# The last FFN block of an attention, MoE and FFN kernel: squares on VectorE, other places for weight splits, g splits and token rows

## The chip, the cores and the metric

The kernel runs on one core of a Trainium2 chip. The metric is device time in microseconds of one execution; lower is better. Engines are called PE (TensorE), DVE (VectorE), ACT (ScalarE), POOL (GpSimd) and SP (SyncE, which here only issues transfers).

## What is computed

Three stages follow one another: windowed attention with 8 heads over 4 x 576 tokens, a top-2 mixture of 8 experts over the 2304 rows of 512, and an FFN over the same rows:

```python
def _moe2_ref(x, w_in, w_out):       # x: 2304 x 512, w_in: 512 x 2048, w_out: 2048 x 512
    h = x @ w_in
    r = np.maximum(h, 0.0)
    g = r * r
    return (g @ w_out).astype(np.float32)
```

In the mixture, each row goes through two experts `relu(x @ w1[e]) @ w2[e]` and the two results are added with weights; this sum is the x of the FFN.

## The kernel before

A float32 product is made of three passes over two parts of each operand: a high part (a rounded copy) and a low part (operand minus high part). Making these two parts is called a split: ACT writes the high part, DVE or POOL the low part. The FFN's two products use a scheme with seven products of sums and differences in place of eight; P1 to P7 name them.

**FFN's first product** runs over three blocks `s` of 768 rows, and in each over eight pairs `k` of column groups. A pair is seven products (`mul_in`, line 968), each of six matmuls of 384 columns. Their order is P1, P2, P6, P5, P7, then P3 of the pair before (`finish_c`, line 1075), then P4. PE adds P1, P6, P7 and P4 into one PSUM tile `a`; ACT reads it between them (lines 1088, 1094, 1099, and 1107 with its relu), and the next product into `a` waits for the read. `g_sum` (line 989) adds an ACT copy to another PSUM tile on DVE (line 991), takes relu and square, and sends the piece to DRAM (`gmid`). In the last block the relu and square of the sums with `q` 2 and 3 are two ACT instructions (lines 993, 994); all others are one DVE instruction (line 996). There are three PSUM tiles with tag a, two with tag b, one with tag c, handed out in turn.

**Work beside it** is put down by step: `step()` (line 1068) runs after each seventh of a pair and does what `on(slot, ...)` registered. 56 slots make a block, and `end` is the slot after the last block. In the last block this is:

- `w_sums(k, 1)` (line 817), the output weights of pair `k`, in six steps: own copy (ACT, 768 columns), own subtraction (DVE), two additions (DVE), two additions (DVE), rest copy (ACT), rest subtraction (POOL) with the next load of raw weights on SP, which waits for it. Line 1055 places them. They overwrite the input weights of the same pair, already used.
- `g_load`, `g_adds`, `g_split` (lines 1005 to 1030): the first batches of g rows for the second product. A batch is loaded from DRAM, POOL makes four sums, and four parts of a split (ACT, DVE, ACT, DVE) write it into one of three places (`GC`) that held the x operands of the first product. Part 1 also issues the load of the batch three later. Lines 1063 to 1065 place the parts of batches 0 and 1.

**FFN's second product** (`mul_out`, line 1120): 36 batches, each two pairs of seven products of three matmuls with 256 columns; a step follows each product. The output weights of pairs 6 and 7 and further g batches are still being split during its first four batches.

**The last expert** stands ahead of the first block. Its first product (`mm1_a`, eight steps `f`) and second product (`mm2`, row tiles `j` 2 to 4) have the FFN's first rows between them: `ygather` (POOL fetches a row tile's two expert results from DRAM), `combine` (ACT scales one, DVE adds the other), `x2_in` (PE transposes, ACT writes). Dictionaries `C_AT` (by `f`, line 943) and `M_AT` (by step of `mm2`, line 954) place them. `y_out` (line 736) copies an output sum from PSUM; the sums are in tiles of tag b, as are the transposes of `x2_in(..., "b")`.

The order on each engine is that of the program: nothing is reordered, and an instruction that waits holds up all behind it on its engine.

Of the kernel before, what the change touches and what calls it, by code (L numbers as in the profile page):

```python
# [16 lines left out]
AF = mybir.ActivationFunctionType  # L17
OP = mybir.AluOpType
# [30 lines left out]
def attn_moe_ffn(ctx: ExitStack, tc: tile.TileContext, qt, kt, vt, wgn, noise, w1, w2, w_in, w_out,  # L49
                 consts, out):  # L50
    nc = tc.nc
# [10 lines left out]
    slots = dram.tile([NS + 2 * N, 1], I32, name="slots")  # L62
# [8 lines left out]
    def bank(tag):  # L71
        if tag == "b":
            return psum.tile([128, 2, 512], F32, name="psb", tag="b", bufs=2)
        return psum.tile([128, 512], F32, name="ps" + tag, tag=tag, bufs={"a": 3, "c": 1}[tag])
# [408 lines left out]
    def out_a(e, f):  # L483
        relu(PA.pop(f), HA[e][:, f, 0, :], HA[e][:, f, 1, :])
# [21 lines left out]
    for p in range(NT // 2):  # L506
        v = 4 * p + 3
        end = v == last
# [85 lines left out]
    for g in range(4):  # L594
        for d in range(4):
            k, q = 4 * (g % 2), (0, 1, 3, 2)[2 * (g // 2) + d // 2]
            pieces.append((w_in[d * 128:(d + 1) * 128, g * 512:(g + 1) * 512],
                           win32[k:k + 4, :, q, d % 2, :].rearrange("k p n -> p k n"), 4))
    for c in range(16):
        q = slice(0, 4, 3) if c < 8 else slice(1, 3)  # L600
# [50 lines left out]
    def ygather(i):  # L651
        for k in range(2):
            YR[i, k] = rows.tile([128, DM], F32, name="yr", tag="r", bufs=6)
            nc.gpsimd.indirect_dma_start(  # L654
                out=YR[i, k], out_offset=None, in_=yg,
                in_offset=bass.IndirectOffsetOnAxis(ap=pos[:, i, k:k + 1], axis=0))
# [71 lines left out]
    def mm2(e, j, f, py):  # L728
        wc = chunks[8 * e + 4 + f // 2]
        wsl = slice((f % 2) * 512, (f % 2) * 512 + 512)  # L730
        b, m = in_b(e, j)
        h = (HB if b else HA)[e][:, f, :, m * 128:(m + 1) * 128]
        for n, (hq, wp) in enumerate(((0, 0), (0, 1), (1, 0))):
            nc.tensor.matmul(py, h[:, hq], wc[wp][:, wsl], start=(f + n == 0), stop=(f == 7 and n == 2))  # L734
# [22 lines left out]
    def settle(*names):  # L757
        for n in names:
            if n == "wb":
                t = lay("wb")  # L760
                WP[0:2] = [[(0, spot(t, 3584 * m, 7))] for m in range(2)]
            elif n == "xb":
                late["xb"] = lay("xb", F32)
                late["xq"] = late["xb"].rearrange("p (q h c n) -> p q h c n", q=2, h=2, c=2)
            elif n == "wc":
                late["wc"], late["ex"] = lay("wc"), lay("ex")
                at_ = [(late["wc"], m) for m in range(5)] + [(late["ex"], m) for m in range(2)]
                for m, (t, o) in zip((0, 1, 5, 3, 6, 4, 2), at_):
                    XC[m] = t[:, 1536 * o:1536 * (o + 1)].rearrange("p (s c n) -> p s c n", s=2, c=2)
            elif n == "tt":  # L770
                tt, wt = lay("tt", F32), lay("wt", F32)
                tmp.extend([tt[:, 0:HALF], tt[:, HALF:2 * HALF], wt[:, 0:HALF], wt[:, HALF:2 * HALF],
                            late["et"][:, 0:HALF], tt[:, 2 * HALF:3 * HALF]])
            else:
                hb, ha, wa = late["hb"], big["ha"], big["wa"]
                WP[2] = [(0, spot(hb, 0, 7))]
                WP[3] = [(0, spot(big["xa"], 0, 6)), (6, spot(hb, 3584, 1))]
                WP[4] = [(0, spot(ha, 0, 7))]
                WP[5:7] = [[(0, spot(wa, 3584 * m, 7))] for m in range(2)]
                WP[7] = [(0, spot(ha, 3584, 5)), (5, spot(wa, 7168, 2))]  # L780
# [36 lines left out]
    def w_sums(k, out_w, own="dve", rest="pool"):  # L817

        i = 64 + 8 * out_w + k
        st = {}  # L820

        def begin():
            load_to(i + 1)
            r = raws.pop(i).rearrange("p (q n) -> p q n", q=4)
            q = [r[:, n, :] for n in range(4)]
            st["own"], st["add"] = split(WP[k], 0, [r[:, 0:3, :]], own), adds(not out_w, q, q, "dve")
            st["rest"] = split(WP[k], 3, [r], rest)
            do(st["own"][0])

        def end():  # L830
            do(st["rest"][1])
            load_to(i + 3)

        return [begin, lambda: do(st["own"][1]), lambda: do(st["add"][:2]), lambda: do(st["add"][2:]),
                lambda: do(st["rest"][0]), end]
# [104 lines left out]
    settle("xb")  # L940
    for i in range(3):
        ygather(i)
    C_AT = {4: [(combine, 0)], 5: [(x2_in, 0, "b"), (ygather, 3), (combine, 1)],
            6: [(x2_in, 1, "b"), (ygather, 4), (combine, 2)], 7: [(x2_in, 2, "b"), (ygather, 5)]}
    for f in range(8):
        mm1_a(last, f)
        out_a(last, f)
        for g, *a in C_AT.get(f, []):
            g(*a)
        for _ in range(1 + f % 2):  # L950
            if wq:
                wq.pop(0)()
    settle("wc")
    M_AT = {1: [(combine, 3)], 2: [(x_hi, 0)], 3: [(x2_in, 3), (x_lo, 0, "dve")], 4: [(combine, 4)], 5: [(x_hi, 1)],
            6: [(x2_in, 4), (x_lo, 1, "dve")], 8: [(combine, 5)], 10: [(x2_in, 5)], 11: [(x_early, 6)],
            12: [(x_early, 5)], 13: [(x_hi, 5)], 14: [(x_early, 3), (x_lo, 5, "dve")], 15: [(x_hi, 3)],
            16: [(x_lo, 3, "dve"), (x_hi, 6)], 17: [(x_early, 4), (x_lo, 6, "dve")], 19: [(x_hi, 4)],
# [1 line left out]
    for j in range(2, NJ):  # L959
        py = bank("b")[:, 0, :]  # L960
        for f in range(8):
            mm2(last, j, f, py)
            for g, *a in M_AT.get(8 * (j - 2) + f, []):
                g(*a)
# [13 lines left out]
    NSB = N // SB  # L978

    def g_to(s, k, q, t):  # L980
        nc.sync.dma_start(out=gmid[s, k, :, :, q, :].rearrange("u p n -> p u n"),
                          in_=t.rearrange("p (u n) -> p u n", u=3))

    def g_tile():
        ng[0] += 1
        n = (ng[0] - 1) % 4
        return tmp[4 + n // 2] if n % 2 == 0 else rows.tile([128, DM], F32, name="yo", tag="yo", bufs=2)[:, 0:HALF]

    def g_sum(s, k, q, ps, u):
        t = g_tile()  # L990
        nc.vector.tensor_tensor(out=t, in0=ps, in1=u, op=OP.add)  # L991
        if s == NSB - 1 and q:
            nc.scalar.activation(out=t, in_=t, func=AF.Relu)
            nc.scalar.activation(out=t, in_=t, func=AF.Square)
        else:
            nc.vector.scalar_tensor_tensor(out=t, in0=t, scalar=0.0, in1=t, op0=OP.max, op1=OP.mult)
        g_to(s, k, q, t)


# [34 lines left out]
    def on(slot, f, *a):  # L1034
        side.setdefault(slot, []).append((f, a))

    def on_all(slots, steps):
        for m, f in zip(slots, steps):
            on(m, f)
# [3 lines left out]
    for s in range(NSB - 1):  # L1043
        for i in range(6):
            t, m = 6 * (s + 1) + i, 56 * s + 5 * i + 3
# [9 lines left out]
    out_sums = [w_sums(k, 1) for k in range(8)]  # L1055
    end = 56 * NSB
    for k in range(7):
        on_all([end - 56 + 7 * (k + 1) + 6 + m for m in (0, 1, 2, 3, 5, 6)], out_sums[k])
    for n in range(3):
        on(end - 35 + n, g_load, n)  # L1060
        for m in range(2):
            on(end - 20 + 4 * n + 2 * m, g_adds, n, "pool", m)
    for n, m in enumerate((-4, -2)):
        for p in range(4):
            on(end + m + p + (p > 1), g_split, n, p)
    slot = [0]

    def step():
# [10 lines left out]
    for s in range(NSB):  # L1079
        for k in range(8):  # L1080
            a = bank("a")[:, :HALF]
            b = bank("a")[:, :HALF]
            c = bank("b")[:, 0, :HALF]
            t, u3, u2 = tmp[0], tmp[1], tmp[2 + k % 2]
# [50 lines left out]
    for n, (s, u, kk) in enumerate(batches):  # L1135
        if kk == 0:
            if (n // 4) % 2:
                t = [bank("b") for _ in range(2)]
# [90 lines left out]
```

## Time and profile before

| | |
|---|---|
| median of 3 runs | 1030.13 us (1024.29 to 1030.23) |
| profiled execution | 1027.78 us, span of its instructions 1026.0 us |
| PE busy | 975.7 us, 95% of the span |
| DVE busy | 680.0 us, 66% |
| ACT busy | 479.8 us, 47% |
| POOL busy | 381.7 us, 37% |
| mean granted PE clock | 0.987 |

The profiled execution's time holds its span and what lies around it. A row of a timeline gives start, duration, engine, line, operation, output and input, count, and in brackets how long the engine had been idle and what it waited for. Rows of one engine can overlap a little, since instructions are pipelined: the distance between starts is the better measure. PEld is PE's weight load, which runs beside its matmuls.

### The profile page before, as it was taken

What the parts mean: (1) busy time and instruction counts of PE and PEld (TensorE: products, weight loads), DVE (VectorE), ACT (ScalarE), POOL (GpSimd) and SP (SyncE); (2) the same over time, 40 slices, a digit from 0 to 9 for tenths busy, and PEclk for the clock granted to TensorE, in tenths of its full rate; (3) what the DMA queues carried; (4) which work ended last, traced back from release to release, by engine and by line L of the source; (5) the groups of instructions that cost most, each with busy time, mean ns of one, the idle gap of its engine ahead of it and who ended that gap; (6) DMA issues with size and microseconds to landing.
All of it is one profiled execution on the core that took longest, in us unless ns stands there. A gap on an engine that the chain in (4) does not pass through costs nothing. (4 is left out here: it accounts for less than half of the span.)

```text
span 1026.0 us, 19586 instructions
## 1 busy us (share of the span) xinstructions
PE 975.7 (95%) x7432; PEld 895.7 (87%) x7432; DVE 680.0 (66%) x1592; ACT 479.8 (47%) x889; POOL 381.7 (37%) x374
## 2 busy tenths in 40 slices
PE   8899789999999999999999989999997879999998
PEld 5677668989898989989898878899997869999998
DVE  5787854557667575757565356976474579987773
ACT  5677652434344443344343246654556574343331
POOL 1444534113121221203130053615121549997880
PEclk9999999999999999999999999999999999999999
DMA  9676422455756565655645252766535453444431
GB/s 324 195 251 237 160 93 93 137 174 180 223 176 172 169 221 175 218 181 181 220 163 161 87 182 82 226 171 185 143 104 161 138 158 110 144 124 145 131 117 42
DMA packets 135733, 168.04 MB, mean 164 GB/s; under 512 B 9856, under 2 KB 96016, under 8 KB 135248
## 3 DMA queue, kind: packets, MB, share of 16 engines
q1 hardware_dynamic: 128160, 145.98, 45.1%
q0 software_dynamic: 7472, 20.76, 6.6%
q8 instruction: 59, 0.97, 0.4%
q14 instruction: 42, 0.34, 0.1%
HBM read 118.69 MB, written 48.01 MB: 162 GB/s over the span
## 5 line engine op out<-in xcount | busy, mean ns | idle before, releaser
L272 ACT ACTIVATE p<-p,mx 128x192 f32<-128x192 f32 x144 | 60.4, 452 | 45.7 <-DVE mx L266 43.8
L815 POOL TENSOR_TENSOR gs<-xb 128x256 f32<-128x256 f32 x72 | 72.1, 1021 | 17.7 <-DVE wc L815 10.6
L472 ACT ACTIVATE ha<-psa 128x384 fp32r<-128x384 f32 x64 | 31.3, 491 | 97.2 <-PE psa L468 95.7
L633 POOL TENSOR_TENSOR ex<-ex 128x512 f32<-128x512 f32 x16 | 20.8, 1302 | 147.7 <-DVE ex L631 147.7
L633 POOL TENSOR_TENSOR et<-ex,et 128x512 f32<-128x512 f32 x16 | 20.9, 1305 | 136.3 <-DVE ex L631 136.3
L473 DVE SCALAR_TENSOR_TENSOR ha<-psa,ha 128x384 fp32r<-128x384 f32 x64 | 35.3, 554 | 49.2 <-ACT ha L472 48.8
L654 POOL DMA_INDIRECT yr<-yg,pos x36 | 38.3, 1065 | 73.9 <-DVE ha L473 52.2
L266 DVE CUSTOM_DVE_ANT_0 p<-psb,bias 128x192 f32<-128x192 f32 (+3 forms) x192 | 58.1, 319 | 9.3 <-PE psb L256 7.1
L424 POOL DMA_INDIRECT slots<-tok,pos x36 | 35.2, 977 | 73.3 <-DVE rs L318 47.3
L468 PE MATMUL psa<-xa,wa 128*128 128x384 f32 x288 | 54.2, 337 | 0.5 <-DVE ha L473 0.3
L738 ACT ACTIVATE yo<-psb 128x512 f32<-128x512 f32 x38 | 22.7, 597 | 67.3 <-PE psb L734 46.2
L468 PE MATMUL psa<-xa,wc 128*128 128x384 f32 x288 | 53.3, 336 | 0.0
L734 PE MATMUL psb<-wa,ha 128*128 128x512 f32 x216 | 52.8, 396 | 0.0
L468 PEld LDWEIGHTS psa<-xa,wa 128*128 128x128 f32 x288 | 49.5, 188 | 1.4 <-DVE ha L473 0.6
L468 PEld LDWEIGHTS psa<-xa,wc 128*128 128x128 f32 x288 | 49.6, 188 | 0.2
L815 DVE TENSOR_TENSOR wc<-gs,wc 128x512 fp32r<-128x512 f32 x48 | 48.8, 1055 | 1.3 <-ACT wc L815 1.3
L734 PEld LDWEIGHTS psb<-wa,ha 128*128 128x128 f32 x216 | 39.5, 188 | 7.8
L734 PE MATMUL psb<-wb,ha 128*128 128x512 f32 x176 | 46.3, 397 | 0.0
L437 POOL DMA_INDIRECT xr<-xd,gidx x40 | 38.4, 960 | 17.2 <-issue 10.3
L114 DVE TENSOR_TENSOR wa<-raw,wa 128x1024 fp32r<-128x1024 f32 x20 | 24.5, 1224 | 29.0 <-ACT wa L110 29.0
L473 DVE SCALAR_TENSOR_TENSOR hb<-psa,hb 128x512 fp32r<-128x512 f32 x32 | 22.1, 691 | 32.1 <-ACT hb L472 32.1
L307 PE MATMUL psb<-v,pt 64*64 64x65 f32 (+1 forms) x1056 | 41.4, 234 | 0.0
(306 smaller groups left out, 2725.8 us busy)
## 6 DMA issues: line engine op xcount, KB each, us to landing
raw<-in_w_dram SPq DMA_DIRECT2D x64, 512.0 KB, 5.3
xb<-gmid SPq DMA_DIRECT2D x72, 256.0 KB, 3.4
v<-in_vt_dram SPq DMA_DIRECT2D x20, 520.0 KB, 5.1
yg<-yo SPq DMA_DIRECT2D x40, 256.0 KB, 3.5
gmid<-yo SPq DMA_DIRECT2D x48, 192.0 KB, 2.1
ex<-in_w_in_dram SPq DMA_DIRECT2D x16, 512.0 KB, 4.9
ex<-in_w_out_dram SPq DMA_DIRECT2D x16, 512.0 KB, 4.3
xd<-xi SPq DMA_DIRECT2D x18, 256.0 KB, 2.5
```

Source lines behind the costliest of these rows:

```text
L266: nc.vector.tensor_tensor_reduce(out=p2[j][p0:p1, a, c0:], in0=ps[p0:p1, a, j, c0:], in1=bias[p0:p1, 4 * g + 2 * j + a, c0:], op0=OP.add, ...
L272: nc.scalar.activation(out=p2[j][:, a, :], in_=p2[j][:, a, :], func=AF.Exp, bias=mx[j][:, a:a + 1], scale=-1.0)
L307: nc.tensor.matmul(px[64 * x:64 * x + 64, a, j, :], l, r, start=not any(m[:2] == (x, a) for m in mms[:n]), stop=not any(m[:3] == (x, a, j) ...
L424: st = nc.gpsimd.indirect_dma_start(out=slots, out_offset=bass.IndirectOffsetOnAxis(ap=pos[:, i, k:k + 1], axis=0), in_=tok[:, i:i + 1], i ...
L437: nc.gpsimd.indirect_dma_start(out=XR[e, j], out_offset=None, in_=xd[0:EARLY * 128] if early else xd, in_offset=bass.IndirectOffsetOnAxis( ...
L468: nc.tensor.matmul(o, w[wp][:, f * 128:(f + 1) * 128], x[:, xp, d, :], start=(n == 0), stop=(n == 11))
L472: nc.scalar.activation(out=hi, in_=ps, func=AF.Relu)
L473: nc.vector.scalar_tensor_tensor(out=lo, in0=ps, scalar=0.0, in1=hi.bitcast(F32), op0=OP.max, op1=OP.subtract)
L633: nc.gpsimd.tensor_tensor(out=cf, in0=af, in1=cf, op=OP.add)
L654: nc.gpsimd.indirect_dma_start(out=YR[i, k], out_offset=None, in_=yg, in_offset=bass.IndirectOffsetOnAxis(ap=pos[:, i, k:k + 1], axis=0))
L734: nc.tensor.matmul(py, h[:, hq], wc[wp][:, wsl], start=(f + n == 0), stop=(f == 7 and n == 2))
L815: f(**a)
```

## The change

Four edits, all of them in or around the FFN's last block:

1. `g_sum` takes relu and square on DVE in all blocks.
2. Steps 1 to 4 of each `w_sums(k, 1)` with `k` below 7 come one slot later, so that the first stands after P1 of pair `k + 2` instead of after P4 of pair `k + 1`. Steps 5 and 6 stay.
3. The four parts of batch 0's g split come at slots -5, -4, -4, -3 from the end of the block instead of -4, -3, -1, 0; batch 1's stay.
4. `combine`, `x2_in` and `ygather` of the last expert's phase come one `f` later; the last of them move from `f` 7 to the first step of `mm2`.

```diff
-    C_AT = {4: [(combine, 0)], 5: [(x2_in, 0, "b"), (ygather, 3), (combine, 1)],
-            6: [(x2_in, 1, "b"), (ygather, 4), (combine, 2)], 7: [(x2_in, 2, "b"), (ygather, 5)]}
+    C_AT = {5: [(combine, 0)], 6: [(x2_in, 0, "b"), (ygather, 3), (combine, 1)],
+            7: [(x2_in, 1, "b"), (ygather, 4), (combine, 2)]}
...
-    M_AT = {1: [(combine, 3)], 2: [(x_hi, 0)], ...
+    M_AT = {0: [(x2_in, 2), (ygather, 5)], 1: [(combine, 3)], 2: [(x_hi, 0)], ...
...
-        if s == NSB - 1 and q:
-            nc.scalar.activation(out=t, in_=t, func=AF.Relu)
-            nc.scalar.activation(out=t, in_=t, func=AF.Square)
-        else:
-            nc.vector.scalar_tensor_tensor(out=t, in0=t, scalar=0.0, in1=t, op0=OP.max, op1=OP.mult)
+        nc.vector.scalar_tensor_tensor(out=t, in0=t, scalar=0.0, in1=t, op0=OP.max, op1=OP.mult)
...
-        on_all([end - 56 + 7 * (k + 1) + 6 + m for m in (0, 1, 2, 3, 5, 6)], out_sums[k])
+        on_all([end - 56 + 7 * (k + 2) + m for m in (0, 1, 2, 3, 4, 5)], out_sums[k])
...
-    for n, m in enumerate((-4, -2)):
-        for p in range(4):
-            on(end + m + p + (p > 1), g_split, n, p)
+    for n, slots in enumerate(((-5, -4, -4, -3), (-2, -1, 1, 2))):
+        for p, m in enumerate(slots):
+            on(end + m, g_split, n, p)
```

## Rows read from the trace of the kernel before

**Rows 1.** Windows by stage: stretch, length, busy us (instructions) by engine, PE clock, DMA share, GB/s

```profile
756.80:832.84 76.04, 62.36 (x337) 59.55 (x337) 41.34 (x70) 43.89 (x84) 26.74 (x20) 0.98 0.49 138
832.84:859.65 26.81, 22.48 (x170) 21.84 (x169) 23.89 (x26) 16.05 (x28) 19.67 (x14) 0.94 0.51 142
859.65:1026.00 166.35, 161.44 (x1346) 161.23 (x1344) 122.44 (x138) 60.72 (x100) 125.50 (x123) 1.00 0.38 119
```

**Rows 2.** Timeline of PE, last block: start, us, what; in brackets idle before

```profile
764.23 3.71 PE L972 MATMUL psa<-wc,wb 128*128 128x384 f32 x18
...
784.99 1.31 PE L972 MATMUL psa<-wc,xa 128*128 128x384 f32 x6 [2.09 <-ACT tt L1088]
786.14 1.20 PE L972 MATMUL psb<-wc,xa 128*128 128x384 f32 x6
787.18 1.20 PE L972 MATMUL psa<-wc,hb 128*128 128x384 f32 x6
...
794.63 1.31 PE L972 MATMUL psa<-wc,ha 128*128 128x384 f32 x6 [2.08 <-ACT tt L1088]
```

**Rows 3.** Timeline of ACT, one pair of the last block

```profile
789.54 0.53 ACT L993 ACTIVATE et<-et 128x384 f32<-128x384 f32 x1 [0.62 <-DVE et L991]
...
790.52 1.04 ACT L815 ACTIVATE wb<-raw 128x1024 fp32r<-128x1024 f32 x1
...
793.37 0.83 ACT L815 ACTIVATE hb<-raw 128x768 fp32r<-128x768 f32 x1
794.11 0.47 ACT L1088 ACTIVATE tt<-psa 128x384 f32<-128x384 f32 x1
```

**Rows 4.** Groups of DVE and POOL in that pair: busy us, mean ns, idle before

```profile
L815 DVE TENSOR_TENSOR raw<-raw 128x256 f32<-128x256 f32 x4 | 1.7, 425 | 0.1
...
L815 DVE TENSOR_TENSOR hb<-raw,hb 128x768 fp32r<-128x768 f32 x1 | 1.0, 959 | 4.2 <-ACT hb L815 4.2
L996 DVE SCALAR_TENSOR_TENSOR yo<-yo 128x384 f32<-128x384 f32 x1 | 0.6, 557 | 0.0
...
L991 DVE TENSOR_TENSOR et<-psb,tt 128x384 f32<-128x384 f32 x1 | 0.6, 556 | 0.6 <-ACT tt L1099 0.6
...
L815 POOL TENSOR_TENSOR wb<-raw,wb 128x1024 fp32r<-128x1024 f32 x1 | 2.4, 2359 | 7.3 <-ACT wb L815 7.3
```

**Rows 5.** Timelines of DVE, POOL and PE, first block

```profile
646.02 2.17 DVE L996 SCALAR_TENSOR_TENSOR yo<-yo 128x384 f32<-128x384 f32 x1
...
645.14 2.64 POOL L815 TENSOR_TENSOR ha<-raw,ha 128x1024 fp32r<-128x1024 f32 x1 [2.35 <-ACT ha L815]
...
664.50 1.31 PE L972 MATMUL psa<-wc,ha 128*128 128x384 f32 x6 [0.96 <-ACT tt L1088]
```

**Rows 6.** Timelines of DVE and POOL, last block, where POOL adds g batches

```profile
817.29 3.60 DVE L815 TENSOR_TENSOR raw<-raw 128x256 f32<-128x256 f32 x4
...
814.77 2.14 POOL L815 TENSOR_TENSOR gs<-xb 128x256 f32<-128x256 f32 x2
...
821.58 0.74 POOL L815 TENSOR_TENSOR gs<-xb,gs 128x256 f32<-128x256 f32 x1
```

**Rows 7.** Timelines of PE and POOL, first four out batches

```profile
837.00 0.50 PE L1122 MATMUL psa<-wb,wc 128*128 128x256 f32 x2 [3.29 <-ACT wc L815]
...
857.87 0.86 PE L1122 MATMUL psa<-wa,wc 128*128 128x256 f32 x5 [0.24 <-POOL wa L815]
...
855.82 2.00 POOL L815 TENSOR_TENSOR wa<-raw,wa 128x512 fp32r<-128x512 f32 x1
```

**Rows 8.** Timelines of PE and DVE, last expert

```profile
604.02 0.66 PE L670 MATMUL psb<-cst,yr 128*128 128x128 f32 x4 [1.35 <-DVE yr L661]
...
611.73 0.66 PE L670 MATMUL psb<-cst,yr 128*128 128x128 f32 x4 [2.23 <-DVE yr L661]
612.14 3.01 PE L734 MATMUL psb<-wa,ha 128*128 128x512 f32 x12
...
610.92 0.75 DVE L661 SCALAR_TENSOR_TENSOR yr<-yr,wts 128x512 f32<-128x512 f32 x1 [3.04 <-DMA yr<-yg,pos]
```

More of the change, by code (lines that the diff above doesn't have):

```diff
@@ L953, in attn_moe_ffn @@
     settle("wc")
-    M_AT = {1: [(combine, 3)], 2: [(x_hi, 0)], 3: [(x2_in, 3), (x_lo, 0, "dve")], 4: [(combine, 4)], 5: [(x_hi, 1)],
+    M_AT = {0: [(x2_in, 2), (ygather, 5)], 1: [(combine, 3)], 2: [(x_hi, 0)], 3: [(x2_in, 3), (x_lo, 0, "dve")], 4: [(combine, 4)], 5: [(x_hi, 1)],
             6: [(x2_in, 4), (x_lo, 1, "dve")], 8: [(combine, 5)], 10: [(x2_in, 5)], 11: [(x_early, 6)],
```

## The prediction

> **What bounds the kernel now.** I read the windows by stage first [rows 1]. TensorE is the engine that counts: from 859.65 us on it is busy 161.44 of 166.35 us, so only a stage in which it waits has something to give. In FFN's last block (756.80 to 832.84) it is busy only 62.36 of 76.04 us, and in the first four out batches behind it 22.48 of 26.81. The granted clock there is 0.98 and 0.94 of its upper level (2.4 GHz), behind them 1.00: a little of the loss is time at the lower level (1.2 GHz), in stretches that follow such waits.
>
> Second, TensorE's timeline in the last block [rows 2]. A pair is seven products of six matmuls, and where nothing is waited for each takes 1.04 us, 7.28 for the pair. Yet the sixth products of two neighbouring pairs start at 784.99 and 794.63, 9.64 apart, each after a wait of about 2.1 us for ScalarE's copy in line 1088. Why is that copy late? ScalarE's timeline of this period [rows 3] answers: from 789.54, where it had waited for VectorE's sum, to the end of that copy at 794.58 it works without a gap, 5.04 us. In its queue stand two squares of two instructions each (lines 993 and 994; 0.98 us from the start of the first to 790.52), the "rest" copy of the output weights (1.04), the own copy of the next weights (0.83, at 793.37) and then the copy that TensorE waits for. The loop is 4.55 us (784.99 to 789.54) of three products, a ScalarE copy and VectorE's sum, then 5.04 us of ScalarE: 9.6 us. VectorE meanwhile idles 4.2 us before its subtraction [rows 4].
>
> The stage as a whole: from 764.23 [rows 2] to 832.84 [rows 1] stand seven pairs and one last product, 7 x 7.28 + 1.04 = 52.0 us of matmuls in 68.6 us. So 16.6 us is waiting, restarts and slow clock. Behind it, 168 matmuls of 0.12 us need 20.16 us and take 26.81 [rows 1]: 6.65 us over, of which 3.29 before 837.00 [rows 7].
>
> **The squares (line 989).** 16 sums lose two ScalarE instructions and gain one VectorE instruction of 0.56 us [rows 4]. Per pair ScalarE loses 2 x 0.98 = 1.96 us between P7 and line 1088. VectorE gains 1.1 us: three sums 1.7, three squares 1.7, subtraction 0.96, four additions 1.7 [rows 4], some 6.1 us of the 7.28.
>
> **The output weights (line 1055).** The first four of six steps come one seventh later, the last two stay. The own copy (0.83 us) goes from before line 1088's copy to behind it; it releases 0.74 us of the chain. Its subtraction and additions come a step later, so the distance from the additions to the rest copy shrinks by a step. Count from the end of a pair's P1: own copy done at 1.3, first sum and square at 2.2, subtraction at 3.2, additions at 5.0, rest copy 5.0 to 6.0, fourth product done at 6.2. ScalarE's copy of line 1088 is then done at 7.8, and the sixth product of the next pair wants it at 8.3. So TensorE would be the bound, with half a microsecond to spare. The loads of raw weights stay at the last step and wait there, as before, for GpSimd's subtraction; no DMA is added, and what is queued behind it on SP is wanted a pair later.
>
> What eats the spare half? GpSimd's subtraction of 2.36 us [rows 4] starts when the rest copy is done, just as VectorE comes to the square of the held sum. In the first block this same meeting is in the trace: the square at 646.02 takes 2.17 us instead of 0.56 while GpSimd's operation begun at 645.14 runs [rows 5]. That is 1.6 us more, so VectorE's loop is 7.7 us against 7.28. The bounds: 0 if the two miss each other, 1.6 a pair if they meet. TensorE's waits in the first block, with squares on VectorE and the same weight work, are at most 0.96 us a pair [rows 5]; nearer to that, I take 0.4 us each for four pairs, 1.6 us. From the fifth pair on GpSimd also has three batches of four additions at about 1.05 us, 12.6 us in all. There four additions of VectorE took 3.60 us instead of 1.7 [rows 6]. Following the queues with 3.0 and 3.4 for these: in the fifth pair the additions end at 6.2, the rest copy (1.2 us there) at 7.4, line 1107's read at 7.9, and the next pair's second product, which takes over that tile, wanted it at 7.3: 0.65 us. A pair later they end 1.7 us after TensorE's need by the same count, 1.6 us of wait; and the last product waits 0.9 for VectorE to have read its tile. Together 3.2 us. The block keeps 16.6 - 1.6 - 3.2 = 11.8 us. Between 0 and all: the end without any meeting is 16.6.
>
> One rule speaks against moving work here. The Trainium skill, SBUF — State Buffer, section "SBUF: two separate sides", says that VectorE and GpSimd share a port pair that is locked exclusively for the whole instruction, so that the loser blocks. The stretched square agrees (2.17 us, ending after GpSimd's). What the rule would make of the additions is a rival below.
>
> **The first g splits (line 1063).** Batch 0's four parts come 1 to 3 steps earlier, all before the last pair's fifth step. Their ScalarE work (0.83 and 1.13 us) then lies beside the sixth pair's products, and the wait of 3.29 us at 837.00 [rows 7] goes with most of what follows it. But the next thing is late: VectorE's queue. It has to do, in the first 18 us of out batches, the same subtractions and additions as before plus one square. By the queue, counted from the first out matmul: a stretched square ends at 1.0, the first half of batch 0's last part at 1.9, wanted at 0.7 (1.2 us of wait); then the whole of it, two sums with squares, batch 1's own part, a weight subtraction and two additions, and the first half of batch 1's last part at 8.2, wanted at 5.8 + 1.2 (1.2 us); batch 3's, behind pair 7's additions, at 19.5, wanted at 18.2 (1.3 us); and GpSimd's two operations for pair 7 (3.6 us, of which the second is in [rows 7]) at 23.9, wanted at 22.1 (1.9 us). There TensorE waited before too, until 857.87 [rows 7]. Sum 5.6 in place of 6.65: 1.05 us gained. Bounds: 6.65 gained if nothing is late, 3.2 lost if two of VectorE's squares there are stretched by 1.6 as well. GpSimd alone has some 35 us of work (six subtractions of 2.36, twenty additions of 1.05 [rows 4, 6]) from the third weights to pair 7's, in the 41 us that TensorE needs for this stretch if it never waits: there is little to win beyond.
>
> **The token rows (lines 943 and 954).** Before, TensorE waited 1.35 us for the first row tile and 2.23 for the third [rows 8]. The third waits for data: VectorE's combine sat 3.04 us until a gather landed [rows 8]. Moved one product later, the first wait shrinks to about 0.4: TensorE gets 2.08 us of matmuls ahead of it, but VectorE now takes the combine behind two other instructions. The third transposes at a landing time that doesn't move, so what is won there is what TensorE does ahead of it: the three matmuls of one step of the second product, 12 of which take 3.01 us [rows 8], so 0.75 us. The third tile's transposes go to the PSUM tile of tag c, which nothing else wants then; the two others stay in tag b, and the next output sum takes a tile read long before. The gathers of the later rows wait for the same buffers and shift with TensorE. Net 0.75 us gained; bounds 0.5 lost (the first wait stays as long as it is, and the row behind it slips) and 1.9 gained (the gather lands 1.2 us earlier, since the raw load ahead of it does).
>
> **Sum.** 11.8 + 1.05 + 0.75 = 13.6 us off 1027.78, the profiled execution's own time: 1014.2. That execution lies 2.35 us under the median of the runs, so by the median it would be 1016.5; I give 1015.
>
> **Rivals.** (a) Nothing meets: all 16.6 and 6.65 gone and 0.75 of the rows, 1003.8 us. For it: GpSimd's operations may fall between VectorE's. Against: those 35 us of GpSimd work in 41. (b) VectorE blocked outright becomes the bound from the fifth pair on: each of its additions waits for a whole GpSimd addition, 0.74 us [rows 6], so four take 4 x (0.43 + 0.74) = 4.7 instead of 3.0 to 3.6. In two pairs and two sets behind them that is some 6 us more on the path: 1020 by the profiled execution, 1022 by the median. For it: VectorE is busy 23.89 of 26.81 us there already [rows 1]. Against: 3.60 was measured. (The exclusive lock in the Trainium skill's SBUF — State Buffer, named above, would make this of it.) (c) Slower: both moved squares are starved in every pair. With 2.0 us more for each and contended additions (3.6) VectorE's loop is 6.1 + 4.0 + 1.9 = 12.0 us; it decides above 9.64. Six pairs at +2.4 give 1027.8 + 14.4 = 1042.2. Against: one GpSimd operation a pair, and one starved square a pair in the first block [rows 5].
>
> **Chances.** Forecast 0.60 (1010 to 1018), (a) 0.14, (b) 0.21, (c) 0.05. From these: faster by over 1% 0.72, within 1% 0.23, slower 0.05; 1% (10.3 us) is about what a measurement of this kernel can tell from no change. The range 1006 to 1024 takes in most of (a) and (b) and leaves out (c).
>
> **What would show it.** Right: TensorE's waits for line 1088 in the last block gone, pairs 7.3 to 7.8 us apart, ScalarE with gaps there, VectorE nearly full, squares of line 996 of over 2 us beside GpSimd's; the wait at the first out batch under 1.5 us. In the last expert's phase still about 3 us of TensorE waiting, now behind the second product's first step. Wrong: pairs still 9 us or more apart, or an out stage longer than 26.8 us that takes the gain back.

## The result and the profile after

The changed kernel takes 1018.13 us (median of 10 runs, 1016.34 to 1023.14), the kernel before on the same chip 1029.01 us (1024.29 to 1032.85): a ratio of 0.990, 95% interval 0.988 to 0.992. It is about 1% faster. The profiled execution takes 1018.73 us with a span of 1016.9, against 1027.78 and 1026.0.

The windows by stage of the kernel after, cut where those of before were cut [rows 1], with the last expert's phase ahead of them (columns as there):

```profile
591.07:630.01 38.94, 37.11 (x193) 32.13 (x192) 25.24 (x42) 21.39 (x37) 14.20 (x13) 1.00 0.43 138
756.34:823.28 66.94, 61.44 (x338) 59.59 (x337) 56.81 (x83) 33.21 (x59) 28.73 (x21) 0.97 0.55 157
823.28:850.60 27.32, 22.38 (x170) 20.60 (x170) 25.45 (x30) 12.18 (x20) 17.29 (x14) 1.00 0.48 138
850.60:1016.90 166.30, 161.43 (x1346) 161.23 (x1344) 122.42 (x138) 60.72 (x100) 125.52 (x123) 1.00 0.38 119
```

| stage | before | after | difference | predicted |
|---|---|---|---|---|
| last expert, from its last eight first-product steps to the FFN | 40.50 | 38.94 | -1.56 | -0.75 |
| FFN's last block | 76.04 | 66.94 | -9.10 | -11.8 |
| first four out batches | 26.81 | 27.32 | +0.51 | -1.05 |
| the rest behind them | 166.35 | 166.30 | -0.05 | 0 |

The stages ahead of the last expert are untouched and took 1.08 us more in this one execution; with that the differences make up the 9.1 us of the span. So the gain is the last block's, and of that block 2.7 us less came than I forecast. (The profile of e2, further down, is of a run that was slow as a whole; no ratio has such runs in it.) In it VectorE went from 41.34 to 56.81 us busy and ScalarE from 43.89 to 33.21: the work changed engines as meant.

TensorE's timeline after, last block and out batches (start, us, what, idle before):

```profile
771.08 3.28 PE L972 MATMUL psa<-wc,hb 128*128 128x384 f32 x18
778.36 3.28 PE L972 MATMUL psa<-wc,xa 128*128 128x384 f32 x18
...
788.07 1.33 PE L972 MATMUL psa<-wc,ha 128*128 128x384 f32 x6 [0.18 <-ACT tt L1084]
...
797.80 2.29 PE L972 MATMUL psa<-wc,wa 128*128 128x384 f32 x6 [2.15 <-ACT tt L1084]
...
815.62 1.31 PE L972 MATMUL psa<-wc,ha 128*128 128x384 f32 x6 [1.49 <-ACT tt L1084]
...
822.11 1.33 PE L972 MATMUL psb<-ex,ha 128*128 128x384 f32 x6 [1.02 <-DVE et L991]
...
825.36 0.99 PE L1118 MATMUL psa<-wb,wc 128*128 128x256 f32 x4 [0.97 <-DVE wc L815]
...
831.95 0.99 PE L1118 MATMUL psa<-hb,wc 128*128 128x256 f32 x4 [1.06 <-DVE wc L815]
...
838.62 0.39 PE L1118 MATMUL psa<-ha,ex 128*128 128x256 f32 x1 [0.52 <-DVE ex L815]
...
845.12 0.99 PE L1118 MATMUL psa<-wa,wc 128*128 128x256 f32 x4 [1.57 <-DVE wc L815]
...
848.83 0.86 PE L1118 MATMUL psa<-wa,wc 128*128 128x256 f32 x5 [0.82 <-POOL wa L815]
```

(The file is four lines shorter: line 1088's copy is now 1084, the copies of P6 and P7 1090 and 1095, the relu and square of a sum 992, the second product's matmul 1118, the relu of P4 1103. Pairs are counted as in the prediction, the first of the seven from 763.78; "the sixth product" there is P6, the third in order.) The wait of 2.1 us in each pair [rows 2] is gone from most of the block: the first pairs start 7.30, 7.28, 7.27 and 7.77 us apart, where 7.28 is the matmuls alone. Then the fifth pair takes 11.20 us, with the wait of 2.15 at 797.80 in it, the next 7.28 again, and the last one with its extra product 11.40 instead of 8.32. Not all of the 11.20 is waiting: behind the wait two products take 2.29 and 1.76 us, at a granted clock of 0.56 in the mean, so mostly at the lower level (window, columns as above):

```profile
797.80:801.48 3.68, 3.68 (x12) 3.68 (x13) 3.51 (x5) 1.17 (x2) 1.92 (x3) 0.56 0.99 271
```

The repetition of this kernel, below, has the same wait (2.04) with products of 1.31 and 1.20 us behind it, so the slow clock cost about 1.5 us here. The block before had such a stretch as well (2.24 and 1.88 us behind the wait at 804.28), so the two compare alike.

Almost all that was not won lies in two places. The second is about what I forecast. The first is not, and the chain of waits around it shows what it is (start, us, what; SPq is SP issuing a transfer, DMA the transfer until it has landed):

```profile
786.60 2.43 DVE yo L992
...
789.04 0.36 SPq L981
...
789.50 0.50 SPq L97
...
790.10 6.12 DMA gmid<-tt
...
796.32 0.50 ACT tt L1103
...
797.27 0.48 ACT tt L1084
```

VectorE's square of the held sum is starved: 2.43 us instead of 0.56. SP has that piece's write to DRAM next in its queue and waits for it. Behind it stand the next load of raw weights (line 97, 512 KB) and then the write of a tile `tt` to DRAM (192 KB), which so starts at 790.10 and lands 6.12 us later. ScalarE's relu of P4 (line 1103) wants to overwrite that tile and waits; behind it, in ScalarE's queue, stands the copy of line 1084, and TensorE waits for that. ScalarE's timeline has the wait itself:

```profile
796.32 0.49 ACT L1103 ACTIVATE tt<-psa 128x384 f32<-128x384 f32 x1 [2.38 <-DMA gmid<-tt]
```

The square is starved by GpSimd's subtraction (timelines of VectorE and GpSimd after):

```profile
778.83 2.44 DVE L992 SCALAR_TENSOR_TENSOR yo<-yo 128x384 f32<-128x384 f32 x1
...
786.60 2.42 DVE L992 SCALAR_TENSOR_TENSOR yo<-yo 128x384 f32<-128x384 f32 x1
...
794.42 2.40 DVE L992 SCALAR_TENSOR_TENSOR yo<-yo 128x384 f32<-128x384 f32 x1
...
786.21 2.39 POOL L815 TENSOR_TENSOR wb<-raw,wb 128x1024 fp32r<-128x1024 f32 x1 [5.36 <-ACT wb L815]
```

One such square comes in each pair, 7.77 and 7.82 us apart.

That the write is issued late is only a part of it. The `tt` writes of the pairs before and behind, in the same place of the queue (782.28 and 797.83), land 4.2 us after their issue, this one 6.12. The trace marks the landing of each transfer in 16 parts: 15 of this one are there at 794.90 and the last at 796.22. In that time the DMA engines also load instructions, which they do beside neither of the two neighbours (rows of the DMA queues, 790.10 to 796.30: packets, MB, share of 16 engines; a packet is 16 KB on q8 and 8 KB on q14):

```profile
q8 instruction: 1, 0.02, 1.0%
q14 instruction: 2, 0.02, 0.9%
```

In the 14 profiles of this case nine writes of `tt` in the last block take over 5 us, and each has an instruction load of 16 KB in flight; without one the longest takes 4.6. Others have one in flight and take no longer. No run moves these loads, so that they hold up the last part is likely and not shown.

### The profile page after: what moved, and what is told of

Same layout as the page of the kernel before. It is cut to its first block, busy times and chain, and to the rows that moved or that the text cites. A ratio compares the mean times of both kernels' runs of the same rounds, so it can differ in the third digit from the quotient of the medians.

```text
span 1016.9 us, 19557 instructions
## 1 busy us (share of the span) xinstructions
PE 975.9 (96%) x7432; PEld 895.6 (88%) x7432; DVE 696.9 (69%) x1608; ACT 465.3 (46%) x857; POOL 381.8 (38%) x374
## 5 line engine op out<-in xcount | busy, mean ns | idle before, releaser
L992 DVE SCALAR_TENSOR_TENSOR yo<-yo 128x384 f32<-128x384 f32 x48 | 43.2, 900 | 1.6
```

## The experiments

Two theories stood at the start. One: the leftover wait comes from the loads of g rows, which share SP's queue with the write that is late. Its rival: it comes from the order in that queue itself, a starved square ahead of a raw load ahead of the write. The first three runs take the edits apart, so that it is seen which of them carries the gain. The runs were made on three chips. On two of them (one had e1 to e4; the other e6, e11, e12 and the repetition) the stages ahead of the FFN take 4 to 6% longer in every profile (652 to 670 us instead of 627 to 630), at a granted clock of 0.93 to 0.97 instead of 0.98, so ratios go with the kernel before on the same chip, and stages are compared from the FFN on.

Lengths in us, last block and first four out batches, from one profile each; TensorE's waits in the two together; its granted clock in each; and the ratio to the kernel before with its 95% interval:

| kernel | block | out | sum | waits | clock | ratio |
| --- | --- | --- | --- | --- | --- | --- |
| before | 76.04 | 26.81 | 102.85 | 17.8 | 0.98, 0.94 | 1 |
| after | 66.94 | 27.32 | 94.26 | 10.4 | 0.97, 1.00 | 0.990 (0.988 to 0.992) |
| after, once more | 66.18 | 27.36 | 93.54 | 11.1 | 1.00, 1.00 | 0.989 (0.984 to 0.994) |
| e1, squares alone | 65.95 | 28.27 | 94.22 | 10.0 | 1.00, 0.88 | 0.988 (0.980 to 0.997) |
| e2, weights alone | 74.31 | 27.55 | 101.86 | 15.4 | 0.98, 0.88 | 0.997 (0.993 to 1.001) |
| e3, token rows and g splits alone | 76.08 | 25.41 | 101.49 | 17.3 | 0.98, 1.00 | 0.997 (0.993 to 1.001) |
| e4, after, g loads early | 66.19 | 27.81 | 94.00 | 11.6 | 1.00, 1.00 | 0.984 (0.977 to 0.991) |
| e5, after, g loads and additions early | 67.66 | 27.59 | 95.25 | 11.3 | 0.97, 1.00 | 0.987 (0.982 to 0.992) |
| e6, after without the g splits | 65.35 | 28.10 | 93.45 | 10.1 | 1.00, 0.94 | 0.993 (0.989 to 0.997) |
| e8, after, write ahead of raw load | 65.94 | 27.05 | 92.99 | 9.6 | 1.00, 0.94 | 0.989 (0.985 to 0.994) |
| e9, e8 and e5 | 65.13 | 27.04 | 92.17 | 8.5 | 1.00, 0.94 | 0.986 (0.981 to 0.990) |
| e10, after, rest subtractions on VectorE | 62.88 | 26.33 | 89.21 | 6.6 | 1.00, 0.94 | 0.984 (0.980 to 0.988) |
| e11, e10 and e8 and e5 | 61.78 | 26.34 | 88.12 | 5.8 | 1.00, 0.94 | 0.987 (0.982 to 0.991) |
| e12, e10 and e8 | 62.74 | 26.31 | 89.05 | 7.4 | 1.00, 1.00 | 0.985 (0.979 to 0.991) |

After and its repetition lie 0.76 us apart in the block and 0.72 in the sum, so a difference of less than about 1 us between two rows says little. And a clock below 1.00 means that a part of the stretch ran at the lower level, which comes and goes from one execution to the next (the change's block has 0.97, its repetition's 1.00). Where I lean on a difference, the waits stand beside it.

**e1: the squares alone.** The kernel before with edit 1 of the diff only.

> The kernel before with the squares alone on VectorE. If ScalarE's queue sets the pace of the last block (my account): its chain between P7 and line 1088's copy loses 1.96 us of 5.04, so the waits of about 2.1 us fall below 0.5 and the block's 76.0 us go to 67 to 69; the whole run is 7 to 9 us faster. If the placement of the output weights is what matters and the squares only move work about: less than 3 us faster. The first out batches stay near 26.8 us in both.

Windows and TensorE's timeline of e1:

```profile
793.68:859.63 65.95, 60.72 (x337) 57.91 (x337) 55.11 (x83) 31.61 (x57) 28.32 (x21) 1.00 0.56 159
...
818.62 1.31 PE L972 MATMUL psa<-wc,xa 128*128 128x384 f32 x6 [0.21 <-ACT tt L1084]
...
836.11 1.31 PE L972 MATMUL psa<-wc,wa 128*128 128x384 f32 x6 [2.17 <-ACT tt L1084]
```

The early pairs wait 0.21 us, though the own copy of the weights still stands ahead of the copy that TensorE wants. The wait of 2.17 is there too, and its chain is the one above (a square of 2.19 us at 824.22, then a write of `tt` that takes 6.30 from 827.50). In block and out batches together this edit alone gives 8.6 us of the change's 8.6. The block is even shorter than expected; the out batches are 1.46 longer than before and not the same, 0.5 of it waits and the rest at a clock of 0.88.

**e2: the output weights alone.** Edit 2 only.

> The kernel before with the output weights alone one seventh later, squares left on ScalarE. If ScalarE's queue sets the pace, 0.74 us leave the chain in each of six pairs: waits of about 1.4 instead of 2.1 us, the block at 71 to 73 us, the run 3 to 5 us faster. If the wait was due to VectorE or the transfers: no change within 1 us.

TensorE's timeline of e2:

```profile
824.69 1.32 PE L972 MATMUL psa<-wc,xa 128*128 128x384 f32 x6 [1.36 <-ACT tt L1088]
```

The wait falls from 2.1 to 1.36 us: 0.7 is the own copy of 0.83 that is now behind [rows 3], as worked out. The block gives 1.7 us and not 3 to 5: in the last two pairs the waits grow, from 2.18 and 3.33 us to 2.69 and 3.95. The out batches are 0.74 longer at a lower clock, with 0.6 us less of waits. The time can't be told from no change.

**e3: token rows and g splits alone.** Edits 3 and 4.

> The kernel before with the two other edits alone: token rows one product later, batch 0's g split earlier; they act in different stages. Last expert (from its last eight products to the FFN's first block): 40.5 us go to about 39 us by the trace of the changed kernel, 39.75 by my prediction. First four out batches: with ScalarE still full in the last pairs the wait of 3.29 us shrinks by 1 to 3 us if it was the order of the splits, and the block ahead grows by up to 2 us, since two ScalarE copies now stand in the last pair; if VectorE's queue sets this stage anyway, its sum with the block doesn't change by more than 1 us. Whole run 1 to 4 us faster.

Window of e3's out batches:

```profile
863.66:889.07 25.41, 21.65 (x169) 20.47 (x169) 22.25 (x24) 15.16 (x26) 20.49 (x14) 1.00 0.49 146
```

The block is as before, the out batches 1.4 us shorter. But only 0.6 of that are waits (3.76 us instead of 4.33); the rest is TensorE's clock, 1.00 here and 0.94 before. The wait of 3.29 us at the first out batch falls to 1.27, and new ones of 0.30 and 1.39 come behind it. The last expert's phase takes 41.11 us, against 41.65 and 41.68 in e2 and e1 on the same chip.

**e6: the change without the g splits.** Edit 3 undone.

```diff
-    for n, slots in enumerate(((-5, -4, -4, -3), (-2, -1, 1, 2))):
-        for p, m in enumerate(slots):
-            on(end + m, g_split, n, p)
+    for n, m in enumerate((-4, -2)):
+        for p in range(4):
+            on(end + m + p + (p > 1), g_split, n, p)
```

> The changed kernel with batch 0's g split back where it was before. If VectorE's queue sets the out stage (my account, and what the two other edits alone showed): block and out stage together (66.9 + 27.3 = 94.3 us in the changed kernel) change by less than 1 us, what one gives the other takes. If the place of the split is a gain of its own: their sum grows by 2 us or more, with a wait of 3 us at the first out batch.

By the table the out batches are 0.74 longer than in the repetition of the change and the block 0.83 shorter, each about what two profiles of one kernel differ by; the sum is the same, 93.45 and 93.54. So with the squares on VectorE no gain of the earlier splits is seen in the stages. VectorE has the same work in the two stretches together, 82.91 us here and 82.26 in the change.

**The repetition.** The unchanged kernel after, on that chip.

> The changed kernel itself, for comparison with the three others on the same chip: block 66.9 and out stage 27.3 us within 0.5, about 10 to 11 us faster than before.

1046.24 us, where the kernel before takes 1056.41. Its block is 0.76 us shorter than the change's, a little more than the 0.5 expected, its out batches the same.

**e4: the g loads elsewhere.** The change, with the loads of the first three g batches at slots -50, -46 and -42.

```diff
-        on(end - 35 + n, g_load, n)
+        on(end - 50 + 4 * n, g_load, n)
```

> The changed kernel with the loads of the first three g batches at slots -50, -46 and -42 from the block's end, in the first three pairs, instead of -35 to -33. In the changed kernel these 1.5 MB, the raw weights and the g pieces fall together between 780 and 796 us; line 1103's relu then waits 2.38 us for the transfer out of the tile that it writes, and TensorE 2.15 us. If this collision is the cause: both waits vanish, and with them about 1.5 us at the lower clock, so the block goes from 66.9 to 63 us and the run is 3 to 4 us faster than the changed kernel (about 14 us faster than before). If the tile is late because the pair has become short and SP's queue stands behind the raw weights: the wait stays at over 1 us, and nothing is gained.

Timelines of TensorE and ScalarE and the chain of waits of e4:

```profile
838.51 1.31 PE L972 MATMUL psa<-wc,wa 128*128 128x384 f32 x6 [2.02 <-ACT tt L1084]
...
837.03 0.49 ACT L1103 ACTIVATE tt<-psa 128x384 f32<-128x384 f32 x1 [2.30 <-DMA gmid<-tt]
...
830.84 6.09 DMA gmid<-tt
```

The loads of g rows are some pairs away and the wait is still there, with the same chain of waits and a write that takes the same 6.1 us. The first theory falls. The instruction loads are there too: one of 16 KB at 834.62, and of the write's 16 parts the last lands 1.8 us behind the others. (The time is 1046.58 us against 1062.35; by the intervals it can't be told from the change's.)

**e8: the write ahead of the raw load.** The change, with the sixth step of each weight set one seventh later. That step issues the raw load, which then stands behind the write of `tt` in SP's queue.

```diff
-        on_all([end - 56 + 7 * (k + 2) + m for m in (0, 1, 2, 3, 4, 5)], out_sums[k])
+        on_all([end - 56 + 7 * (k + 2) + m for m in (0, 1, 2, 3, 4, 6)], out_sums[k])
```

> The changed kernel with the last step of each weight set (GpSimd's subtraction and SP's load of raw weights) one seventh later, behind P4's relu, so that the transfer of tile tt stands ahead of the 512 KB of raw weights on SP. Account A, SP's order: tt's transfer is issued some 0.5 us earlier and lands in 2 to 4 us instead of 6; line 1103's wait of 2.4 us and TensorE's of 2.15 before the sixth pair vanish; from the starved squares alone stay waits up to 0.5 us a pair; block 66.9 to 63 or 64 us. Account B, the starved square alone: the transfer of yo ahead of it still waits for the square, TensorE's wait in pair 5 stays over 1 us, block over 66 us. In the out stage GpSimd takes the second half of batch 3's additions ahead of pair 6's subtraction: 0 to 1 us.

DMA issues of the last block, after and then e8 (KB each, median us from issue to landing):

```profile
gmid<-yo SPq DMA_DIRECT2D x16, 192.0 KB, 2.1
...
gmid<-tt SPq DMA_DIRECT2D x8, 192.0 KB, 4.1
```

```profile
gmid<-tt SPq DMA_DIRECT2D x8, 192.0 KB, 2.4
```

Chain of waits and timelines of ScalarE and TensorE of e8:

```profile
788.01 4.92 DMA gmid<-tt
...
793.04 0.49 ACT L1103 ACTIVATE tt<-psa 128x384 f32<-128x384 f32 x1 [0.58 <-DMA gmid<-tt]
...
794.51 1.32 PE L972 MATMUL psa<-wc,wa 128*128 128x384 f32 x6 [0.83 <-ACT tt L1084]
...
801.34 0.85 ACT L815 ACTIVATE xa<-raw 128x768 fp32r<-128x768 f32 x1 [2.90 <-DVE raw L815]
...
803.86 1.31 PE L972 MATMUL psa<-wc,wa 128*128 128x384 f32 x6 [1.77 <-ACT tt L1084]
```

As the rival has it, the order moves the landing: in the median a write of 192 KB takes 2.4 us ahead of the 512 KB and 4.1 behind it. At the place that cost most it still takes 4.92, again with an instruction load in flight. ScalarE's wait goes from 2.38 to 0.58 us, 1.2 by the shorter landing and the rest by the earlier issue, and TensorE's from 2.15 to 0.83. But the block wins nothing by it, because a pair later the next thing is late, by 1.77: ScalarE's rest copy waits 2.90 us for VectorE's additions. That is the wait of "a pair later" which the prediction had put at 1.6. In all TensorE waits 5.9 us in this block and 5.4 in the change's; the 1.0 us by which it is shorter is the clock (1.00 and 0.97). So neither account came out: the wait fell below 1 us, and the block is 65.94 us, not 63 or 64.

**e5: g loads and g additions earlier.** The change with

```diff
-        on(end - 35 + n, g_load, n)
+        on(end - 50 + n, g_load, n)
...
-            on(end - 20 + 4 * n + 2 * m, g_adds, n, "pool", m)
+            on(end - 44 + 4 * n + 2 * m, g_adds, n, "pool", m)
```

> The changed kernel with the first three g batches loaded in the first pair of the last block and added by GpSimd from slot -44 on (pairs 2 to 4) instead of slot -20 (pairs 6 and 7). If GpSimd's additions beside VectorE's cost the waits of the last pairs (1.49 before pair 8's sixth product, 1.02 before the last, additions of 3.41 us): those go, block 66.9 to 64 or 65, the out stage 27.3 to 25 or 26 since VectorE's queue ends earlier; the wait of 2 us in pair 5 stays. If VectorE's queue is full without them: no more than 1 us gained in all.

TensorE's timeline of e5:

```profile
788.51 1.34 PE L972 MATMUL psa<-wc,ha 128*128 128x384 f32 x6 [1.52 <-ACT tt L1084]
...
798.15 2.13 PE L972 MATMUL psa<-wc,wa 128*128 128x384 f32 x6 [2.05 <-ACT tt L1084]
```

GpSimd's additions now meet VectorE's some pairs earlier: new waits of 1.14 and 1.52 us come there, the one of 2.05 stays, and the 1.49 of the last pair goes. In all TensorE waits 6.1 us in the block instead of 5.4, and the block is 0.7 longer. The early additions move waits and save none.

**e9: e8 and e5 together.**

> Both: SP's order and the early additions. If the two waits have separate causes, the gains add: block 66.9 to 61 or 62 us (59 is the products alone), out stage 25 to 26, the run 6 to 8 us faster than the changed kernel. If one cause feeds the other: no better than the better of the two alone.

The sum is 92.17 us, 0.8 less than with e8 alone, and the time 1013.54 us against 1028.85. The direction is the other one than in e5, but 0.8 us of one profile each is too little to show it. The block of 61 or 62 us that two separate gains would have made didn't come (65.13).

**e10: no GpSimd beside the squares.** The change, with the rest subtraction of the first six pairs on VectorE instead of GpSimd.

```diff
-    out_sums = [w_sums(k, 1) for k in range(8)]
+    out_sums = [w_sums(k, 1, "dve", "dve" if k < 6 else "pool") for k in range(8)]
```

> The changed kernel with the rest subtraction of the output weights of the first six pairs on VectorE instead of GpSimd. The squares of 2.4 us beside GpSimd's subtraction then have nothing to meet: they fall to 0.56, VectorE's loop is 6.1 + 1.2 = 7.3 instead of 7.8 us. If the starved square feeds the lag that ends in pair 5's wait: waits of the first five pairs under 0.3 us, block 63 to 64. If the lag comes from SP and the transfers alone: the wait of 2 us stays.

Groups of line 992 in the last block, after and then e10 (busy us, mean ns):

```profile
L992 DVE SCALAR_TENSOR_TENSOR yo<-yo 128x384 f32<-128x384 f32 x16 | 18.3, 1142 | 0.5
```

```profile
L992 DVE SCALAR_TENSOR_TENSOR yo<-yo 128x384 f32<-128x384 f32 x16 | 10.4, 649 | 0.6
```

Windows of e10, timeline of VectorE in one pair and, later, where GpSimd adds g batches, TensorE's longest wait, and ScalarE's ahead of it:

```profile
753.51:816.39 62.88, 59.67 (x338) 58.14 (x338) 55.13 (x91) 33.92 (x61) 16.39 (x14) 1.00 0.58 167
...
775.99 0.56 DVE L992 SCALAR_TENSOR_TENSOR yo<-yo 128x384 f32<-128x384 f32 x1
...
776.46 1.22 DVE L815 TENSOR_TENSOR wb<-raw,wb 128x1024 fp32r<-128x1024 f32 x1
...
788.13 3.49 DVE L815 TENSOR_TENSOR raw<-raw 128x256 f32<-128x256 f32 x4
...
794.07 1.32 PE L972 MATMUL psa<-wc,wa 128*128 128x384 f32 x6 [1.75 <-ACT tt L1084]
...
791.65 1.06 ACT L815 ACTIVATE hb<-raw 128x1024 fp32r<-128x1024 f32 x1 [2.96 <-DVE raw L815]
```

VectorE takes the subtractions over and is still busy less in the block, 55.13 us against 56.81: the subtraction costs it 1.22 us, and the squares beside it 0.65 in place of 1.14 in the mean. The block falls by 4.1 us to 62.88 (3.3 against the repetition, which has the same clock), in the first four pairs TensorE no longer waits, and in the last pair 0.18 us instead of 1.49 and 1.02. So what GpSimd's subtractions cost there is shown. What is left is the additions beside GpSimd's: four in 3.49 us, and 1.75 us of wait behind them, in the fifth pair.

No relu waits for a write any more, but in the fifth pair that is not because the write is in time. It takes 5.56 us there (4.0 in the median) and lands at 791.22, 1.0 us after P4 has ended at 790.23; the relu, at 792.61, doesn't notice, since ScalarE stands before its rest copy until 791.65. Nor does e10 tell two waits in SP's queue apart, as it takes both away: that of the piece's write for the starved square, and that of the raw load for GpSimd's subtraction, which in the change ended only 0.42 us before the square (788.60 and 789.02).

**e12 and e11: on top of e10.** e12 is e10 with e8's order; e11 is e12 with e5's loads and additions.

> The changed kernel with the rest on VectorE and SP's order, g batches where they were. If SP's order matters only because a starved square stands ahead: no gain over the rest on VectorE alone (block 62.9, within 0.5 us). If the tile's transfer is late by itself: block 61 to 62.

> The changed kernel with all three: rest subtractions of the first six pairs on VectorE, SP's order, g batches loaded and added early. If the waits left with the rest on VectorE (1.75 us before the sixth pair's product, 0.62 a pair later) come from GpSimd's additions beside VectorE's: they move to pairs 3 and 4 and shrink below 1 us in all, block 62.9 to 60 or 61 us, the run 2 to 3 us faster than with the rest on VectorE alone (1009 to 1010 where before is 1029). If VectorE, at 7.3 us a pair, is simply full: no gain over that kernel.

TensorE's timeline of e11:

```profile
807.66 1.31 PE L972 MATMUL psa<-wc,xa 128*128 128x384 f32 x6 [1.37 <-ACT tt L1084]
```

The order gains nothing here: 89.05 us against 89.21, with 7.4 us of waits against 6.6. With the starved squares the sum fell by 1.3 (94.26 to 92.99), 0.8 of it waits, hardly more than two profiles differ by. What is certain of the order is the one wait that it shortens in e8. Spreading the additions comes with another 0.9 us, within what profiles differ by; a wait of 1.37 us is left. In time e11, e12 and the change's repetition can't be told apart by their intervals. e10 is the version that I would keep: 1012.15 us (1010.88 to 1013.42) against 1028.85 on its chip, where the change took 1018.13 against 1029.01; the intervals of the two ratios just touch at 0.988. By the profiles its block and out batches are 5.05 us shorter than the change's, and 4.33 than the repetition's.

## Why the prediction came out as it did

The forecast was 1015 us, the median is 1018.13, and the sign and what bounds the kernel were right. Some luck is in the total: the block came 2.7 us short and the out batches 1.6, and the token rows gave back 0.8. Of the signs named, TensorE's waits for the copy of P1 are gone in most pairs, but 2.15 and 1.49 us of them are left in two. By its steps:

- **What bounds the block.** Right. ScalarE's squares lay on the path, and e1 shows that they alone carry the gain of block and out batches.
- **The weights.** "It releases 0.74 us of the chain" is what e2 shows by itself (2.1 to 1.36). On top of the squares it shows no gain: squares alone make 94.22 us, the whole change 94.26. Both edits shorten the same queue of ScalarE, and e1 shows that with the squares gone the copy is only 0.21 us late.
- **The starved square.** The mechanism and VectorE's loop are right: 7.7 us forecast, 7.77 and 7.82 measured. "0.4 us each for four pairs, 1.6 us" is too dear: TensorE lost 0.02 us over the first three of these pairs and 0.49 in the fourth.
- **The fifth pair: the step that failed.** Its loss was put at 0.65 us, from VectorE's additions. It was 3.92 us: a wait of 2.15, and some 1.5 of matmuls at the lower clock, which the repetition doesn't have. The wait came by a way that the prediction had ruled out with "what is queued behind it on SP is wanted a pair later". It followed SP's queue as far as the issue and counted no landing time. Each starved square puts VectorE some half a microsecond further behind TensorE (the three above start 0.47, 0.97 and 1.02 us after their pairs), and SP's write of the starved piece, the raw load and the write of `tt` go out that much later. ScalarE wants the tile back 3.84 us after the last of these has been issued, at 790.10. In the pair before it was 3.86, the write took 4.2, and ScalarE waited 0.45: there the lag has already reached TensorE, for 0.49 us. In the fifth pair the write takes 6.12, and the wait is 2.38. So the late issue is shown to cost some half a microsecond a pair, and the leap to 2.15 comes from 1.9 us more of landing, whose cause stays open: instruction loads lie beside it, and the g loads are ruled out by e4.
- **The sixth and seventh pair.** 2.5 us forecast (1.6 and 0.9), 3.08 measured, with waits of 1.49 and 1.02 in it. Right in kind and nearly in size, but not in place: the sixth pair lost nothing (7.28 us), and all of it fell on the seventh. The block as a whole: 0.02 + 0.49 + 3.92 + 3.08 = 7.5 us lost, where 1.6 + 3.2 = 4.8 were forecast; 16.6 - 7.5 is the 9.1 that was won.
- **The out batches: a sum of unlike things.** The waits were forecast one by one as 1.2, 1.2, 1.3 and 1.9 us, 5.6 in all; measured are 0.97, 1.06, 0.52, 1.57 and 0.82, 4.94 in all. So VectorE's queue is the next thing late there, as said. But "5.6 in place of 6.65" compares waits with waits and slow matmuls. Before, the waits alone were 4.33 us (3.29 and 0.24 [rows 7], and 0.80 at 838.30), and the other 2.3 were matmuls slower than 0.12 us, since TensorE was busy 22.48 us [rows 1] and not 20.16: a part of them ran at the lower clock (0.94), and behind a wait four matmuls take 0.99 us. After, it is busy 22.38 at full clock, with more stops. Like against like, my own numbers gave a loss of 1.3 us; measured is a loss of 0.51, with 0.61 more of waits. Counted in waits, the earlier splits alone give 0.6 us (e3) and the squares alone cost 0.5 (e1); the change has both. (The lower bound of the forecast is mis-added, too: 5.6 and twice 1.6 are 8.8, a loss of 2.15 us and not 3.2.)
- **The token rows.** 0.75 us forecast, bound 1.9, measured 1.56 in the one profile; 0.55 on e3's chip. The first wait fell to 0.24 (0.4 forecast). At the third, the premise of "a landing time that doesn't move" was wrong. Timelines of TensorE and VectorE after:

```profile
606.06 0.66 PE L670 MATMUL psb<-cst,yr 128*128 128x128 f32 x4 [0.24 <-DVE yr L661]
...
611.72 0.66 PE L670 MATMUL psc<-cst,yr 128*128 128x128 f32 x4 [1.56 <-DVE yr L661]
...
610.91 0.75 DVE L661 SCALAR_TENSOR_TENSOR yr<-yr,wts 128x512 f32<-128x512 f32 x1 [0.98 <-ACT yr L660]
```

  VectorE's combine no longer sits 3.04 us until a gather lands [rows 8]; the last thing it waits for is ScalarE's scaling, 0.98 us. With the 1.08 us by which this execution was later by then, it starts 1.1 us earlier than before, near the 1.2 of the upper bound. Why the gather landed earlier I have not tested apart from the rest.

**The rivals.** (a), that nothing meets, didn't come; e10, which takes the meeting of GpSimd's subtraction and VectorE's square away, takes 13.2 us off the block, and e11 takes 14.3, where 16.6 was the most. (b) asked for 4.7 us for four additions of VectorE beside GpSimd's; 3.41 was measured at 809.75, and 3.49 in e10. The time lies between my forecast and this rival's 1022, but by another mechanism. (c) asked for two starved squares in each pair; there was one.

The rule of the Trainium skill, SBUF — State Buffer, section "SBUF: two separate sides", that a GpSimd operation holds the shared port pair exclusively, agrees with the squares of 2.40 to 2.44 us, which shrink to 0.56 once no GpSimd operation lies beside them. Beside GpSimd's additions of 256 columns the trace shows less than the rule says: VectorE's take 0.85 us each there instead of 0.43, not the 0.43 + 0.74 of a whole lock.

## What to carry to other kernels

When an instruction is moved to an engine that shares something with a neighbour, price the stretched instruction and then everything that is issued behind it: a transfer whose source it is, and what stands behind that transfer in the same queue, up to the landing and to whoever wants the buffer back. A lag of some tenths per round is free only until the slack of such a buffer is used up (here 0.47 us of lag cost nothing and 0.97 cost 0.49); from then on a transfer that lands late costs all of its delay. And compare waits with waits: the length of a stretch also holds what the clock and the restarts made of it, and two profiles of one kernel differ in that.

## What the runs showed of the hardware

- A write of 192 KB on SP's queue landed 2.1 us after its issue in the median of the `yo` tiles, 4.1 in that of the `tt` tiles behind a load of 512 KB, and 6.1 at the place that cost most here, with g loads shortly before it or without (e4). Ahead of the same load it took 2.4 in the median and 4.9 at that place (e8). At that place one of the write's 16 parts landed 1.1 to 1.8 us after the others in the change, its repetition, e4 and e8, with instructions being loaded at the same time.
- One GpSimd subtraction of 2.39 us stretches a VectorE square of 0.56 us to 2.42, so that moving this subtraction to the fuller engine, for 1.22 us, made that engine's busy time fall (e10).
- The chips differ: the kernel before took 1029, 1056 and 1062 us (medians) on the three, while the change's last block and first out batches took 94.26 us in the profile beside the first of these and 93.54 beside the second.
